# Leftover rows of a spectral mixer in four groups of 32 partitions, and a new order of its column products

## The chip, the cores and the metric

The kernel runs on one core of a Trainium2 chip. The metric is the device time of one execution in microseconds; the time of a kernel is the median over its runs.

## The reference, cut to what matters

```python
x = A_x                                            # [1, 2048, 576], bf16
X = rfft2(layernorm(x), axes=(-2, -1)) * (w_r + 1j * w_i)
h = x + irfft2(X, s=(2048, 576)).astype(bf16)
out = h + (gelu(layernorm(h) @ w_gate) * (layernorm(h) @ w_up)) @ w_down
```

`gelu` is the tanh approximation; `w_gate` and `w_up` are 576 by 4608, `w_down` 4608 by 576. Only the first half, the two-dimensional transform and its inverse, is touched by the change. The second half, the feed-forward network, takes most of the time.

## The kernel before

The 2048 tokens lie as 16 heads h of 128 partitions. All transforms are matmuls with tables that the kernel makes itself. An order written out by hand sets what each engine does: every engine works off its own queue in the order of the program text, and waits where an operand isn't there yet. DMAs are issued by SP's queue. PSUM is one ring of four buffers of two banks each, which all products share (`two`).

**Row transform** (`norms`, `row16`, `rests`). For each head VectorE scales the 128-point row table by the layer norm's 1/std into `FR` (L391), and TensorE multiplies the head's columns by it. The 576 columns are folded into 288 pairs (d, d + 288). `row16` does the pairs 0 to 255 as two full blocks, and adds the mean by a small product with `mneg`. The 32 pairs that are left (columns 256 to 319 and 512 to 575 hold them) go through `rests` (L351): per head two products of 64 columns and two with the mean, in the two halves of the array's columns, 128 wide. `evict` (ScalarE, L361) copies the full blocks of two heads from PSUM to `Bt[:, 0:4]`, `evict4` (L367) the leftovers of four heads to `Bt[:, 4]`, on ScalarE for heads 0 to 7 and on VectorE after that.

**Tables.** `DT` is the column table (sine and cosine, by `col_sin` on ScalarE and `mirror` on VectorE), with block 2 (`D3`) for the leftovers; `DF` is a copy of the parts of it that the leftover products use, with zeros elsewhere. `TF` holds the twiddles (minus sine, cosine, sine) of the second row step, by k. VectorE makes angles (`angle_a`, `angle_b` for the sine, `angle_s`, `angle_c` for the cosine), ScalarE the sine and cosine, VectorE the negated sine. The slice `first` (k = 1, 2) is made early, `rest` (the seven others) after the row transform. `turn_tf` transposes them by DMA into `TI` for the way back; `load_dq` copies `DT` into `DQ` by DMA for the inverse column products.

**Loop over k** (order 1 to 7, then 0). For a column c of the row result, `f2(c)` makes the column products: two output parities, each of three matmuls of 290 columns, two with `DT` and one with `DF` for the leftovers (L550). `f2_out` copies them to `pq` (ScalarE, L561). `f3(k, half)` applies the twiddles to `pq[k]` and `pq[k + 8]` (TensorE L567 and L568, copy to `g` or `hs` on ScalarE L589). `sum_of` (L600) and `wmul` (L618 to L639), both VectorE, form sums and multiply by the spectral weights, giving `Zt`. `i3(k)` is the inverse row product (L658), copied to `EO` by ScalarE. `inv_cols` (L709) and `add_rows` (L848) finish the inverse; then the network's `gate` blocks begin (L978). `wmul` of one k forms the sums of the next k between its own steps.

The order of the loop is software pipelining: step i runs `f2` of its k, `f3` of the k before, `wmul` of the one before that, and `i3` of the third one back. In step 0 the products of k = 1 put the leftover matmuls of both parities last.

Of the kernel before, what the change touches and what calls it, by code (L numbers as in the profile page):

```python
# [20 lines left out]
P = 128  # L21
# [21 lines left out]
def kernel_body(  # L43
# [67 lines left out]
    DF = keep.tile([P, 2, 2, JH], BF16, name="DF")  # L111
# [76 lines left out]
    V.memset(DF[:], 0.0)  # L188
# [18 lines left out]
    iota(iD[64:128, 2:3], [[0, 1]], 2 * P + 64 + 192, 1)  # L207
# [50 lines left out]
    first, rest = slice(0, 2), slice(2, 9)  # L258
# [54 lines left out]
    def fill(dst, n):  # L313

        for _ in range(n):
            T.matmul(dst, lhsT=ident[:], rhs=h_sb[:, 0, 0:512], start=True, stop=True)

    def row16(h):
# [6 lines left out]
        for t in range(2):  # L325
            for n, d0 in ((0, t * P), (1, DH + t * P)):
# [9 lines left out]
                lhsT=mneg[:, 0, h : h + 1].to_broadcast([P, P]),  # L336
# [5 lines left out]
    def rests(h):  # L342
        ps_f["f4", h] = two("f4")
        for i in range(4):
            row16_rest(h + i)

    def row16_rest(h):
        o = (h % 4) * P
        for mean in (False, True):
            for p0, d0 in ((0, 256), (64, 512)):  # L350
                T.matmul(  # L351
                    ps_f["f4", h - h % 4][p0 : p0 + 64, 0, o : o + P],
                    lhsT=mneg[:, 1, h : h + 1].to_broadcast([P, 64]) if mean else h_sb[:, h, d0 : d0 + 64],
                    rhs=FR[:, h, 0, :],
                    start=not mean,
                    stop=mean,
                )
# [8 lines left out]
    def evict4(h):  # L366
        (V.tensor_copy if h >= 8 else A.copy)(  # L367
            Bt[:, 4, :].rearrange("p (c h l) -> p h c l", c=16, h=16)[:, h : h + 4, :, :],
            ps_f["f4", h][:, 0].rearrange("p (h c l) -> p h c l", h=4, c=16),
        )  # L370
# [91 lines left out]
    rests(0)  # L462
# [5 lines left out]
    rests(4)  # L468
# [4 lines left out]
    evict(0, 2)  # L473
    evict4(0)
    evict(4, 6)
    evict4(4)
# [6 lines left out]
    rests(8)  # L483
# [8 lines left out]
    rests(12)  # L492
# [50 lines left out]
    def f2(c):  # L543
# [3 lines left out]
        if c == order[0]:  # L547
            steps.sort(key=lambda s: s[1] == 4)
# [551 lines left out]
```

## Time and profile before

| | us |
|---|---|
| median of 3 runs | 494.45 (494.05 to 494.75) |
| the profiled execution | 494.6 |
| span of its instructions | 492.8 |
| TensorE busy in it | 484.7 |
| VectorE, ScalarE, POOL busy | 223.4, 158.2, 29.5 |
| first column product begins | 21.96 |
| first gate block begins | 65.57 |

The span is the time from the first to the last instruction of the profiled execution. PE is TensorE, DVE VectorE, ACT ScalarE, POOL GpSimd; SPq is the queue that issues DMAs. A line of the order of time gives start, length, engine, line of the kernel, operation, what it writes and reads with its shape, and how many instructions were merged; in brackets stands the idle time ahead of it and what ended that. Matmuls are pipelined, so the lengths of single ones overlap: what one costs in a row of them is the distance from one start to the next. The granted TensorE clock was 1.000 in the whole span.

### The profile page before, as it was taken

What the parts mean: (1) busy time and instruction counts of PE and PEld (TensorE: products, weight loads), DVE (VectorE), ACT (ScalarE), POOL (GpSimd) and SP (SyncE); (2) the same over time, 40 slices, a digit from 0 to 9 for tenths busy, and PEclk for the clock granted to TensorE, in tenths of its full rate; (3) what the DMA queues carried; (4) which work ended last, traced back from release to release, by engine and by line L of the source; (5) the groups of instructions that cost most, each with busy time, mean ns of one, the idle gap of its engine ahead of it and who ended that gap; (6) DMA issues with size and microseconds to landing.
All of it is one profiled execution on the core that took longest, in us unless ns stands there. A gap on an engine that the chain in (4) does not pass through costs nothing.

```text
span 492.8 us, 12868 instructions
## 1 busy us (share of the span) xinstructions
PE 484.7 (98%) x5762; PEld 338.9 (69%) x5762; DVE 223.4 (45%) x457; ACT 158.2 (32%) x280; POOL 29.5 (6%) x84
## 2 busy tenths in 40 slices
PE   6999999999999999999999999999999999999997
PEld 3777789875589955555699755555799655555995
DVE  8999774798622177333311345333121333333111
ACT  8899863322210022332200132332110232232000
POOL 8500010011100011000000000000000000000000
PEclk9999999999999999999999999999999999999999
DMA  8838979769970049966720089876600377760000
GB/s 278 234 74 184 246 115 240 165 128 212 223 161 3 3 118 195 192 145 147 152 65 1 37 170 199 174 145 147 143 3 3 92 158 155 150 146 1 14 13 25
DMA packets 89582, 62.35 MB, mean 127 GB/s; under 512 B 23222, under 2 KB 88118, under 8 KB 89526
## 3 DMA queue, kind: packets, MB, share of 16 engines
q1 hardware_dynamic: 89238, 60.34, 57.5%
q0 software_dynamic: 288, 1.18, 0.7%
q8 instruction: 45, 0.74, 0.7%
q14 instruction: 11, 0.09, 0.1%
HBM read 52.65 MB, written 2.36 MB: 112 GB/s over the span
## 4 chain that ended last, share of the span: by engine, by line
PE 95%; ACT 2%; POOL 1%; DMA 1%; issue 0%; DVE 0%; ACTq 0%; POOLq 0%
PE gu L978 57%; PE acc L1021 27%; PE pq_ps L550 2%; PE cs_ps L709 2%; PE acc L1040 2%; PE eo_ps L658 2%; ACT junk L128 1%; PE y_ps L848 1%; PE gh_ps L568 1%; PE gh_ps L567 1%; DMA h_sb<-in_A_x_dram 1%; POOL rstd L138 1%; ACT Bt L361 0%; POOL wm_r L397 0%; PE eo_ps L682 0%
## 5 line engine op out<-in xcount | busy, mean ns | idle before, releaser
L978 PE MATMUL gu<-Bt,wgu 64*128 64x512 bf16 (+1 forms) x2646 | 270.6, 363 | 0.0
L978 PEld LDWEIGHTS <-wgu 64*128 64x128 bf16 x2646 | 151.5, 94 | 115.6 <-issue 0.3
L987 DVE TENSOR_TENSOR P_sb<-g_sb,gu 128x512 bf16<-128x512 f32 (+1 forms) x156 | 100.4, 645 | 140.3 <-ACT g_sb L986 140.3
L986 ACT ACTIVATE g_sb<-gu 128x512 f32<-128x512 f32 (+1 forms) x156 | 88.0, 564 | 193.5 <-PE gu L978 193.5
L1021 PEld LDWEIGHTS <-P_sb 64*128 64x128 bf16 x2160 | 122.2, 94 | 10.9
L1021 PE MATMUL acc<-wd,P_sb 64*128 64x288 bf16 x1440 | 90.9, 283 | 0.0
L1030 DVE TENSOR_TENSOR part<-part,acc 128x576 f32<-128x576 f32 x15 | 11.3, 754 | 112.6 <-ACT part L1029 112.6
L1029 ACT COPY part<-acc 128x576 f32<-128x576 f32 x15 | 9.6, 639 | 122.8 <-PE acc L1021 122.8
L1021 PE MATMUL acc<-wd_a,P_sb 64*128 64x288 bf16 x720 | 46.8, 283 | 0.0
L550 PE MATMUL pq_ps<-DT,Bt 128*128 128x290 bf16 x64 | 12.3, 286 | 0.7 <-ACT Bt L361 0.7
L978 PE MATMUL gu<-Bt,wgu_e 64*128 64x256 bf16 (+1 forms) x162 | 12.5, 305 | 0.0
L873 DVE TENSOR_SCALAR hrow<-h_sb,mv,rstd 128x1152 bf16<-128x1152 bf16 x14 | 12.2, 868 | 0.6 <-POOL rstd L911 0.6
L138 POOL TENSOR_TENSOR rstd<-rstd,mhalf 128x1 f32<-128x1 f32 (+2 forms) x17 | 12.0, 709 | 1.4
L1032 DVE TENSOR_TENSOR h_sb<-h_sb,part 128x576 bf16<-128x576 bf16 x15 | 11.4, 758 | 0.5
L550 PEld LDWEIGHTS <-Bt 128*128 128x128 bf16 x96 | 9.1, 97 | 3.4 <-ACT Bt L361 0.8
L978 PEld LDWEIGHTS <-wgu_e 64*128 64x128 bf16 x162 | 10.3, 94 | 1.2
L137 POOL TENSOR_SCALAR rstd<-mv 128x1 f32<-128x1 f32 (+2 forms) x17 | 4.1, 242 | 116.7 <-DVE mv L123 116.0
L561 ACT CAST pq<-pq_ps 128x580 bf16<-128x580 f32 x16 | 10.5, 666 | 1.2 <-PE pq_ps L550 1.1
L709 PE MATMUL cs_ps<-DQ,EO 58*128 58x290 bf16 x144 | 10.8, 283 | 0.0
L327 PE MATMUL f2t<-FR,h_sb 128*128 128x256 bf16 x64 | 9.2, 273 | 0.6 <-DVE FR L391 0.6
L709 PEld LDWEIGHTS <-EO 58*128 58x128 bf16 x160 | 7.8, 94 | 2.4 <-issue 0.7
L550 PE MATMUL pq_ps<-DF,Bt 128*128 128x290 bf16 x32 | 8.9, 285 | 0.0
(149 smaller groups left out, 283.9 us busy)
## 6 DMA issues: line engine op xcount, KB each, us to landing
wgu<-in_B_w_gate_dram SPq DMA_DIRECT2D x46, 432.0 KB, 5.1
wgu<-in_B_w_up_dram SPq DMA_DIRECT2D x46, 432.0 KB, 6.1
wd_a<-in_B_w_down_dram SPq DMA_DIRECT2D x1, 1728.0 KB
wd<-in_B_w_down_dram SPq DMA_DIRECT2D x1, 1728.0 KB
wd<-in_B_w_down_dram SPq DMA_DIRECT2D x6, 288.0 KB, 7.9
out_dram<-h_sb SPq DMA_DIRECT2D x3, 576.0 KB
h_sb<-in_A_x_dram SPq DMA_DIRECT2D x4, 288.0 KB, 4.3
h_sb<-in_A_x_dram SPq DMA_DIRECT2D x2, 576.0 KB
```

What stands on the lines that cost most here:

```text
L138: G.tensor_tensor(dst[:, sl], dst[:, sl], mhalf[:, sl], ALU.pow)
L550: T.matmul(ps[:, par, 0:JP], lhsT=Bt[:, t, col], rhs=DT[:, t // 2, par] if t < 4 else DF[:, par], start=(t == par), stop=(t == 4),)
L561: copy(pq[c][:, rs].rearrange("p r (j a) -> p r j a", a=2), pq_ps[c][:, :, 0:JP].rearrange("p a (r j) -> p r j a", r=2)[:, rs],)
L658: T.matmul(pv[:, n], lhsT=z[:, a, w].rearrange("p b j -> p (b j)"), rhs=TI[:, ts[k], 1 - a : 3 - a, :], start=(a == 0), stop=(a == 1),)
L709: T.matmul(ps[:, e, 0:JP], lhsT=EO[x][rows, w, 2 * g : 2 * g + 2].rearrange("p h e k l -> p (h e k l)"), rhs=DQ[rows, w] if w or e else DT ...
L873: V.tensor_scalar(hrow[:], h_sb[:, h, :].rearrange("p (r k) -> p r k", k=64).unsqueeze(2).to_broadcast([P, NR, 2, 64]), mv2[:, h, 0:1], rs ...
L978: T.matmul(gu[:, c, 0:n], lhsT=w[rows, r, i * P : (i + 1) * P], rhs=hl[tcnk % 2][rows, r, lo:hi], start=(r == 0), stop=(r == NR - 1),)
L986: A.activation(g_sb, gu[:, 0, 0:n], ACT.Gelu_apprx_tanh)
L987: V.tensor_tensor(p_sb(f)[:, lo:hi], g_sb, gu[:, 1, 0:n], ALU.mult)
L1021: T.matmul(accs[i][:, c, 0:DH], lhsT=p_sb(f)[rows, st * P : (st + 1) * P], rhs=wd[f // NWA][rows, f % NWA, c * DH : (c + 1) * DH], start=( ...
L1030: V.tensor_tensor(part, part, accs[1][:, :, 0:DH], ALU.add)
L1032: V.tensor_tensor(hv, hv, part, ALU.add)
```

## The change

Leftovers. `rests` now does eight heads at a time and is called twice, after heads 0 to 7 and after 8 to 15. Per head and column parity it forms the 32 leftover pairs in 32 partitions, so that (e, parity) with e = 0 for k and e = 1 for k + 8 fills four groups of 32 partitions; each product is 32 columns by 64. `Bt[:, 4]` keeps half its width; `evict4` copies eight heads at once. `DF` is gone: `D3` holds the same 32 rows in each group. The two last rows of the column table, which `DQ` needs, come from three small ScalarE activations into `edge`, and reach `DQ` by a DMA of their own in each `load_dq`.

Column products. `f2(k)` now does k and k + 8: eight full matmuls, then four leftover matmuls of 32 rows each, one in each group of partitions. For the first k, 32 matmuls of 32 columns are put ahead; `f2` overwrites what they write. 

Order. The products of the first two k come before the first `f3`; then those of the next two before the first `wmul`. From then on a step is `f3`, `f2` of the next k, `i3` of two k back, `wmul`. The late twiddles are made in two parts, k = 3, 4, 5 and k = 6, 7, 0, 8, with the sine and cosine of the second part later and its negated sine inside the first `wmul`. The negation of `G16` moves behind the last `wmul`.

```diff
     V.memset(mhalf[:], -0.5)
-    neg = keep.tile([P, 2], FP32, name="neg")
-    for i in range(2):
-        V.memset(neg[:, i : i + 1], -2.0 + i)
-    mneg = keep.tile([P, 2, H], BF16, name="mneg")
+    mneg = keep.tile([P, H], BF16, name="mneg")
...
     D3 = DT[:, 2]
-    DF = keep.tile([P, 2, 2, JH], BF16, name="DF")
+    edge = Bt[0:2, 4, 8 * P : 8 * P + 4 * JH].rearrange("p (r a j) -> p r a j", r=2, a=2)
     DQ = keep.tile([P, NW, 2, JH], BF16, name="DQ")
...
     def minus_means(lo, hi):
-        sh = [P, 2, hi - lo]
-        G.tensor_tensor(
-            mneg[:, :, lo:hi],
-            mv[:, lo:hi, 0].unsqueeze(1).to_broadcast(sh),
-            neg[:].unsqueeze(2).to_broadcast(sh),
-            ALU.mult,
-        )
+        G.tensor_scalar(mneg[:, lo:hi], mv[:, lo:hi, 0], -2.0, None, op0=ALU.mult)
...
-    V.memset(DF[:], 0.0)
+    for t, b in ((edge[:, 0, 0], hpib), (edge[:, 0, 1], nhpib), (edge[:, 1].rearrange("p a j -> p (a j)"), zerob)):
+        A.activation(t, zerob[0:2].to_broadcast(list(t.shape)), ACT.Sin, bias=b[0:2])
     V.memset(DT[:, :, 1, :, JH - 1], 0.0)
...
     iota(iD[:], [[P, 3]], 0, 1)
-    iota(iD[64:128, 2:3], [[0, 1]], 2 * P + 64 + 192, 1)
+    for p0 in (32, 64, 96):
+        iota(iD[p0 : p0 + 32, 2:3], [[0, 1]], 2 * P, 1)
     iJ = tmp("iJ", [P, 2 * JM], FP32)
...
                 f2t[:, b, t * 2 * P : t * 2 * P + P],
-                lhsT=mneg[:, 0, h : h + 1].to_broadcast([P, P]),
+                lhsT=mneg[:, h : h + 1].to_broadcast([P, P]),
                 rhs=FR[:, h, 0, :],
...
-    def rests(h):
-        ps_f["f4", h] = two("f4")
-        for i in range(4):
-            row16_rest(h + i)
-    def row16_rest(h):
-        o = (h % 4) * P
-        for mean in (False, True):
-            for p0, d0 in ((0, 256), (64, 512)):
-                T.matmul(
-                    ps_f["f4", h - h % 4][p0 : p0 + 64, 0, o : o + P],
-                    lhsT=mneg[:, 1, h : h + 1].to_broadcast([P, 64]) if mean else h_sb[:, h, d0 : d0 + 64],
-                    rhs=FR[:, h, 0, :],
-                    start=not mean,
-                    stop=mean,
-                )
+    def rests(h0):
+        ps = ps_f["f4", h0] = two("f4")
+        for h in range(h0, h0 + 8):
+            o = (h - h0) * 64
+            F = FR[:, h].rearrange("p s (x e n) -> p s x e n", x=2, e=2)
+            for n in range(3):
+                for e in range(2):
+                    for par in range(1 if n == 2 else 2):
+                        p0 = 64 * e + 32 * par
+                        T.matmul(
+                            ps[p0 : p0 + 32, 0, o : o + 64],
+                            lhsT=mneg[:, h : h + 1].to_broadcast([P, 32])
+                            if n == 2
+                            else h_sb[:, h, 256 + DH * n : 288 + DH * n],
+                            rhs=F[:, par if n == 1 else 0, :, e],
+                            start=(n == 0),
+                            stop=(n == 2 - par),
+                        )
...
     def evict4(h):
-        (V.tensor_copy if h >= 8 else A.copy)(
-            Bt[:, 4, :].rearrange("p (c h l) -> p h c l", c=16, h=16)[:, h : h + 4, :, :],
-            ps_f["f4", h][:, 0].rearrange("p (h c l) -> p h c l", h=4, c=16),
+        (V.tensor_copy if h else A.copy)(
+            Bt[:, 4, 0 : 8 * P].rearrange("p (c h l) -> p h c l", c=8, h=H)[:, h : h + 8],
+            ps_f["f4", h][:, 0].rearrange("p (h c l) -> p h c l", h=8, c=8),
         )
...
     norms(0, 4)
-    rests(0)
     minus_sine(first)
...
     norms(4, 8)
-    rests(4)
+    rests(0)
     ln_fin(slice(9, 12, 2))
...
     gather(1)
-    evict(0, 2)
+    evict(0, 2, 4, 6)
     evict4(0)
-    evict(4, 6)
-    evict4(4)
     sd(12, 13)
...
     norms(8, 12)
-    rests(8)
     sd(14, 15)
...
     norms(14, 16)
-    rests(12)
+    rests(8)
     evict(8, 10)
...
     evict4(8)
-    V.tensor_copy(DF[0:32], D3[0:32])
-    V.tensor_copy(DF[96:128], D3[96:128])
-    evict4(12)
     for w, t in ((WR, wm[0]), (WI, wm[1])):
         nc.sync.dma_start(w[:, 9 : H + 1, 0:J], t[:].rearrange("p (r j) -> p r j", r=8))
-    angle_a(rest)
-    angle_b(rest)
+    part_a, part_b = slice(2, 5), slice(5, 9)
+    angle_a(part_a)
+    angle_b(part_a)
+    sine(part_a)
+    angle_s(part_a)
+    angle_c(part_a)
+    minus_sine(part_a)
+    angle_a(part_b)
+    angle_b(part_b)
+    angle_s(part_b)
+    angle_c(part_b)
     for w in (WR, WI):
...
             j0, j1 = w * JW, (w + 1) * JW
-            for lo, hi in ((j0, min(j1, (j0 // P + 1) * P)), ((j0 // P + 1) * P, j1)):
+            for lo, hi in ((j0, min(j1, (j0 // P + 1) * P)), ((j0 // P + 1) * P, min(j1, DH))):
                 if lo < hi:
...
                     )
+        p0 = 64 * r + DH % JW
+        nc.sync.dma_start(DQ[p0 : p0 + 2, NW - 1], edge[:, r])
...
-    def f2(c):
-        ps = two("pq_ps")
-        col = slice(slot[c] * P, (slot[c] + 1) * P)
-        steps = [(par, t) for par in range(2) for t in (par, par + 2, 4)]
-        if c == order[0]:
-            steps.sort(key=lambda s: s[1] == 4)
-        for par, t in steps:
-            T.matmul(
-                ps[:, par, 0:JP],
-                lhsT=Bt[:, t, col],
-                rhs=DT[:, t // 2, par] if t < 4 else DF[:, par],
-                start=(t == par),
-                stop=(t == 4),
-            )
-        pq[c] = wk.tile([P, 2, JP], BF16, name="pq", tag="pq", bufs=6)
-        pq_ps[c] = ps
+    def f2(k):
+        cc = (k, k + 8)
+        for c in cc:
+            ps = pq_ps[c] = two("pq_ps")
+            if c == order[0]:
+                for _ in range(32):
+                    T.matmul(ps[:, 0, 0:32], lhsT=ident[:], rhs=h_sb[:, 0, 0:32], start=True, stop=True)
+            for par in range(2):
+                for t in (par, par + 2):
+                    T.matmul(
+                        ps[:, par, 0:JP],
+                        lhsT=Bt[:, t, slot[c] * P : (slot[c] + 1) * P],
+                        rhs=DT[:, t // 2, par],
+                        start=(t == par),
+                        stop=False,
+                    )
+            pq[c] = wk.tile([P, 2, JP], BF16, name="pq", tag="pq", bufs=6)
+        for e, c in enumerate(cc):
+            col = (slot[c] // 8 * 4 + slot[c] % 4) * P
+            for par in range(2):
+                rows = slice(64 * e + 32 * par, 64 * e + 32 * par + 32)
+                T.matmul(
+                    pq_ps[c][:, par, 0:JP],
+                    lhsT=Bt[rows, 4, col : col + P],
+                    rhs=D3[rows, par],
+                    start=False,
+                    stop=True,
+                )
...
         times(WI, m2, slice(0, J))
+        if i == 1:
+            minus_sine(part_b)
         if k:
...
-    n = len(order)
-    for i in range(n + 1):
-        last = i >= n
-        if not last:
-            f2(order[i])
-            if i != 1:
-                f2_out(order[i])
-        if i == 0:
-            f2(order[0] + 8)
-            f2_out(order[0] + 8)
-            angle_s(rest)
-            angle_c(rest)
-            sine(rest)
-        if 1 <= i <= n:
-            f3(order[i - 1], 0)
-            f3(order[i - 1], 1)
-            if i == 1:
-                f2_out(order[1])
-                minus_sine(rest)
-                sum_of(order[0], 0)
-                sum_of(order[0], 1)
-                V.tensor_scalar(G16v[1], G16v[0], -1.0, None, op0=ALU.mult)
-            else:
-                if i == 2:
-                    cosine(slice(2, 3))
-                elif i == 3:
-                    turn_tf(slice(2, 4))
-                    turn_tf(slice(4, 9))
-                    load_dq(0)
-                    pre = [load_gu(g) for g in range(3)]
-                    nc.sync.dma_start(wd_a[:], wd_view[:, 0:NWA, :])
-                wmul(order[i - 2], i - 1, order[i - 1])
-        if not last and i:
-            f2(order[i] + 8)
-            f2_out(order[i] + 8)
-            if i == 2:
-                cosine(slice(3, 9))
-        if last:
+    def both_out(k):
+        f2_out(k)
+        f2_out(k + 8)
+    o = order
+    f2(o[0])
+    both_out(o[0])
+    f2(o[1])
+    f2_out(o[1])
+    f3(o[0], 0)
+    f2_out(o[1] + 8)
+    f3(o[0], 1)
+    cosine(part_a)
+    turn_tf(part_a)
+    sum_of(o[0], 0)
+    sum_of(o[0], 1)
+    f3(o[1], 0)
+    f3(o[1], 1)
+    sine(part_b)
+    for j in (2, 3):
+        f2(o[j])
+        both_out(o[j])
+    wmul(o[0], 1, o[1])
+    f3(o[2], 0)
+    f3(o[2], 1)
+    cosine(part_b)
+    turn_tf(part_b)
+    load_dq(0)
+    pre = [load_gu(g) for g in range(3)]
+    nc.sync.dma_start(wd_a[:], wd_view[:, 0:NWA, :])
+    scr_pool.__exit__(None, None, None)
+    eop = ctx.enter_context(tc.tile_pool(name="eop", bufs=1, side="right"))
+    EO = [eop.tile([P, 5, H, 2, 4, 8], BF16, name=f"EO{x}", tag=f"EO{x}") for x in range(2)]
+    for s in range(3):
+        i3(o[0], s)
+    wmul(o[1], 2, o[2])
+    for j in range(3, 8):
+        f3(o[j], 0)
+        f3(o[j], 1)
+        if j < 7:
+            f2(o[j + 1])
+            both_out(o[j + 1])
+        else:
             inv_cols(0, 0)
             inv_cols(0, 1)
-        if i >= 3:
-            for s in range(3):
-                i3(order[i - 3], s)
-        if last:
-            wmul(order[i - 1], i)
-        if i == 2:
-            scr_pool.__exit__(None, None, None)
-            eop = ctx.enter_context(tc.tile_pool(name="eop", bufs=1, side="right"))
-            EO = [eop.tile([P, 5, H, 2, 4, 8], BF16, name=f"EO{x}", tag=f"EO{x}") for x in range(2)]
+        for s in range(3):
+            i3(o[j - 2], s)
+        wmul(o[j - 1], j, o[j])
+    wmul(o[7], 8)
+    V.tensor_scalar(G16v[1], G16v[0], -1.0, None, op0=ALU.mult)
     for g in (2, 3, 4):
```

More of the change, by code (lines that the diff above doesn't have):

```diff
@@ L256, in first_a @@
             G.tensor_scalar(pr[:, k], q16[:], s2p[:, 0:1], ks[:, k : k + 1], op0=ALU.mult, op1=ALU.add)
-    first, rest = slice(0, 2), slice(2, 9)
+    first = slice(0, 2)
     first_a()
@@ L315, in fill @@
         for _ in range(n):
-            T.matmul(dst, lhsT=ident[:], rhs=h_sb[:, 0, 0:512], start=True, stop=True)
+            T.matmul(dst[:, 0:512], lhsT=ident[:], rhs=h_sb[:, 0, 0:512], start=True, stop=True)
     def row16(h):
```

## The prediction

> **What bounds the kernel now.** I read the page's busy line first, then the chain of waits, then the stretch that the change rewrites by windows, then each engine's order of time there. All times are microseconds from the span's start.
>
> ```profile
> PE 484.7 (98%) x5762; PEld 338.9 (69%) x5762; DVE 223.4 (45%) x457; ACT 158.2 (32%) x280; POOL 29.5 (6%) x84
> ```
>
> Over the span TensorE is the bound. The change touches only the first 55 us, and these rows show that stretch: the chain (start, length, what), then one window (length; busy time of PE, its weight loads, DVE, ACT, POOL), then VectorE's order of time.
>
> ```profile
> 28.08 1.48 PE pq_ps L550 x12
> 38.06 0.74 PE pq_ps L550 x6
> 38.80 1.09 PE eo_ps L658 x10
> 41.62 0.74 PE pq_ps L550 x6
> 48.01 1.35 PE cs_ps L709 x20
> 49.36 1.20 PE eo_ps L658 x10
> 65.57 27.46 PE gu L978 x468
> ...
> 28.00:48.00 20.00, 19.93 (x167) 15.76 (x167) 20.00 (x46) 19.59 (x35) 0.00 (x0) 1.00 0.68 137
> ...
> 31.07 0.76 DVE L618 TENSOR_TENSOR m<-xab,WR 128x1156 bf16<-128x1156 bf16 x1
> 34.64 0.76 DVE L618 TENSOR_TENSOR m<-xab,WR 128x1156 bf16<-128x1156 bf16 x1
> 48.92 0.76 DVE L618 TENSOR_TENSOR m<-xab,WR 128x1156 bf16<-128x1156 bf16 x1
> ```
>
> The whole-kernel share misleads here. From 28 to 48 TensorE, VectorE and ScalarE are all full. TensorE needs 41.62 - 38.06 = 3.56 for one k; VectorE needs 34.64 - 31.07 = 3.57 for the multiplication of one k and never waits. TensorE finishes each k just behind VectorE: the multiplication of k=6 ends at 48.92 and its inverse product starts at about 49.3 (49.36 in the chain). So a shorter TensorE step shortens the kernel by that lag, 0.3 to 0.4, and no more, unless VectorE also starts earlier.
>
> **Leftover products of the row transform.**
>
> ```profile
> 15.27 0.22 PE L351 MATMUL f<-FR,h_sb 128*64 128x128 bf16 x2
> 15.33 0.22 PE L351 MATMUL f<-FR,mneg 128*64 128x128 bf16 x2
> 15.48 0.39 PE L327 MATMUL f2t<-FR,h_sb 128*128 128x256 bf16 x2
> ...
> 20.22 0.22 PE L334 MATMUL f2t<-FR,mneg 128*128 128x128 bf16 x1
> 20.28 0.38 PE L327 MATMUL f2t<-FR,h_sb 128*128 128x256 bf16 x2
> 20.50 0.22 PE L334 MATMUL f2t<-FR,mneg 128*128 128x128 bf16 x1
> 21.96 0.67 PE L550 MATMUL pq_ps<-DT,Bt 128*128 128x290 bf16 x4 [0.68 <-ACT Bt L361]
> ...
> 19.98 1.93 ACT L361 CAST Bt<-f2t 128x1024 bf16<-128x1024 f32 x2
> ...
> 19.10 0.48 DVE L391 TENSOR_SCALAR FR<-F,rstd 128x256 bf16<-128x256 bf16 x2
> ...
> 47.94 0.29 PE L709 MATMUL cs_ps<-DT,EO 58*128 58x290 bf16 x1
> 47.95 0.80 PE L709 MATMUL cs_ps<-DQ,EO 58*128 58x290 bf16 x9
> ```
>
> A pair in two column halves, 128 columns each, costs 0.06; leaving that mode costs 0.15 - 0.06 = 0.09. Four heads cost 8 x 0.06 + 0.09 = 0.57. After the change eight heads have 24 turns of 64 columns, up to four matmuls each. If four run together as two do (47.94 and 47.95 begin 0.01 apart), a turn is half of 0.06 and a set takes 24 x 0.03 + 0.09 = 0.8. If each of its 80 matmuls takes the 0.03 that one of a pair takes, it is 80 x 0.03 = 2.4. I take 0.8, because the rows show matmuls in different parts starting together; 2.4 is the upper end.
>
> Rows 14 and 15 wait for FR at 19.10, not for TensorE, so the last row product still begins at 20.50. Then comes the second set, 20.65 to 21.4. ScalarE's last row evictions still end at 21.9 (19.98 + 1.93): they wait for row 15. The 32 new small matmuls stand in TensorE's queue ahead of the first column product and wait for nothing. Today there is 0.68 of idle time there to take them. Each streams 32 columns: from 0.014 (1.48 / 12 = 0.123 for 290 columns, scaled) to 0.055 (20.28 - 20.22, a full matmul with its own weight load), so 0.45 to 1.8 in all. I take 0.027 each, half of the upper row, since the streaming is a quarter and the weight load stays: 0.85. The first column product then begins at 21.4 + 0.85 = 22.3, 0.3 later than 21.96 (ends: 0 and +1.2).
>
> **Products of k and k+8 together.** Per k, 12 steps of 0.123 (1.48) become 8 (0.99) and one turn of four matmuls in four row groups. Changing the array's mode costs 1.35 - 10 x 0.123 = 0.12 going in (20 matmuls in pairs), and 1.20 - 1.09 = 0.11 coming out. By the first rows above it is 0.09; I take 0.18 for both ways. Run together, the turn costs 0.12 + 0.18 = 0.30 and a k saves 0.19, 1.5 over eight. Run one by one it is 0.49 + 0.18 and a k loses 0.18. I take the saving. The Trainium skill, "TensorE: Matmul & The Clock Gate", section "Measured speedup vs the span model", gives 3.07 times for four row groups, not 4; by that the turn would cost an estimated 0.04 more, which changes TensorE's work and not the sum below.
>
> **VectorE, which then decides.**
>
> ```profile
> 20.54 0.68 DVE L367 CAST Bt<-f 128x512 bf16<-128x512 f32 x1
> 21.13 0.29 DVE L500 COPY DF<-DT 32x580 bf16<-32x580 bf16 x1
> ...
> 21.77 0.69 DVE L367 CAST Bt<-f 128x512 bf16<-128x512 f32 x1
> 22.50 1.15 DVE L245 SCALAR_TENSOR_TENSOR pr<-q,s2p,ks 128x896 int32<-128x896 f32 x1
> 23.68 0.63 DVE L269 TENSOR_SCALAR pr<-pr 128x896 int32<-128x896 int32 x1
> 24.34 0.73 DVE L272 TENSOR_SCALAR ab<-pr 128x896 f32<-128x896 int32 x1
> 25.11 0.63 DVE L232 TENSOR_SCALAR ab<-ab 128x896 int32<-128x896 int32 x1
> 25.66 0.42 DVE L284 TENSOR_SCALAR TF<-TF 128x896 bf16<-128x896 bf16 x1
> 25.99 1.41 DVE L600 TENSOR_TENSOR xab<-g,gh_ps 128x578 bf16<-128x578 bf16 x2
> 27.32 0.22 DVE L760 TENSOR_SCALAR G<-G 128x256 bf16<-128x256 bf16 x1
> 27.49 0.77 DVE L618 TENSOR_TENSOR m<-xab,WR 128x1156 bf16<-128x1156 bf16 x1
> ...
> 25.29 0.62 ACT L589 CAST g<-gh_ps 128x578 bf16<-128x578 f32 x1
> ```
>
> Gone before the first multiplication are the two DF copies (21.77 - 21.13 = 0.64), one eviction (0.73) and the negation of G (0.17), about 1.5. But the eviction of the leftovers stands first in this queue, and it moves from 20.54 to 21.6, behind the second set. It takes 0.6; the angles, 25.66 - 22.50 = 3.16 in four passes, become eight half passes and one short minus-sine, about 3.7 with their extra starts. VectorE is free for the sums at 21.6 + 0.6 + 3.7 = 25.9, as before (25.99).
>
> The sums also need the first g. TensorE: 22.3, the column products of k=1, 9 and of k=2, 10 (2 x 1.29, from 0.99 + 0.30), the first half of the twiddle product of k=1 (4 x 0.123): 25.4. ScalarE copies it with 0.2 of latency and 0.53 (25.29 to the next start at 25.82): the sums begin at about 26.2 and the first multiplication at 26.2 + 1.33 = 27.5, no earlier than 27.49. In it now stands the minus-sine of the late part (0.26), which needs ScalarE's late sine. ScalarE's queue ahead of it: g to 26.1, the copy of 10, an early cosine (0.5 by its columns), g and hs of k=2, then 0.6 of sine, ending near 29.1, while the second multiplication ends at 27.5 + 1.35 = 28.85. VectorE waits 0.3 and then works 0.26: every later k is 0.5 to 0.6 later on VectorE. TensorE, 0.19 per k shorter, takes back the lag of 0.3 but also ends its last k with a change of mode. **Sum**: +0.55 - 0.3 = +0.25 if all the lag is used, +0.55 if none; I take +0.4.
>
> **Hidden edits.**
>
> ```profile
> 5.98 0.46 DVE L384 BATCH_NORM_STATS2 st<-h_sb 128x6 f32<-128x288 bf16 x1 [0.52 <-DMA h_sb<-in_A_x_dram]
> ...
> 9.72 0.27 POOL L137 TENSOR_SCALAR rstd<-mv 128x4 f32<-128x4 f32 x1 [0.48 <-DVE FR L391]
> ...
> 33.41 4.44 SPq L518 DMA_DIRECT2D DQ<-DT  x6
> ```
>
> Three edge activations on ScalarE delay the first row table by about 0.2; VectorE's wait of 0.52 for input at 5.98 hides it. Two more iotas on POOL, some 0.4, lie ahead of a wait of 0.48 at 9.72; without that cover they would cost 0.4. Two edge DMAs of about 0.74 each (4.44 / 6), and a late twiddle transpose waiting for its cosine, move SP's weight loads by some 4; their first use is at 65.57.
>
> **Rivals.**
> *Leftovers one by one* (slower). The second set takes 2.4 and the first delays rows 8 to 11 by 1.6: the second set ends near 23.9, the leftovers' eviction and the first column product come 2.5 later, +2.9: 497.5. It decides from the point where a matmul of 32 columns by 64 costs over 0.015. For it: no row here shows four column groups. Against it: the pair at 47.94. The Trainium skill, "TensorE: Matmul & The Clock Gate", section "Wait — 56ns, not 53.3ns?", states that start to start never drops below about 25 ns however small N is; by that rule this rival would hold, and the pairs of this trace contradict it for different parts of the array. Chance 0.15.
> *Small matmuls at full price* (slower). 32 x 0.055 = 1.8: the column products begin at 23.2 and the sum is +1.3: 495.9. Against it: three quarters of their streaming is gone. Chance 0.2; smaller delays of the leftovers' eviction end here too.
> *TensorE's saving counts* (faster). If VectorE were free earlier, 8 x 0.19 less: 493.1. For it: 1.5 of VectorE's work before the first multiplication is gone. Against it: 20.00 of 20.00 busy, and nothing removed from its 3.57. Chance 0.1.
> *The change does nothing to the path*: TensorE's lag pays for the late minus-sine, 494.6; part of the forecast.
>
> **How the numbers follow.** The profiled execution took 494.6 with a span of 492.8; the median shown is 494.45, 0.15 less. So 494.6 + 0.4 = 495.0, or 494.9 as a median. About 0.2% (1.0) is what a measurement of this kernel tells from no change. The forecast (chance 0.55) has its own range of 494.3 to 495.5, nearly all of it within 0.2%. With the rivals the range is 494.0 to 497.4. Slower by over 0.2%: 0.15 + 0.2 and a little of the forecast, 0.42. Faster by over 0.2%: 0.1. Within: 0.48.
>
> **What would show it.** Right: VectorE still full from 28 to 48 at 3.57 per k, with small TensorE waits on it; the first column product at 22.0 to 22.4; a VectorE wait for ScalarE's late sine. Wrong: a second leftover set over 1.2 long, a step per k other than 3.57, or a first multiplication before 27.

## The result, and the profile after

| | before | after |
|---|---|---|
| median, us (lowest to highest, 7 runs each) | 494.55 (494.05 to 494.75) | 496.06 (495.67 to 496.67) |
| profiled execution, us | 494.6 | 496.67 |
| span, us | 492.8 | 494.9 |

The ratio is 1.0033, with a 95% interval of 1.0021 to 1.0045: slower by 1.5 us. The forecast was 494.9, with a range of 494.0 to 497.4 that holds the result. The forecast's own part of that range ended at 495.5 and doesn't hold it.

The page of after (busy time of each engine) shows what the whole-kernel view can: almost nothing.

```profile
PE 484.0 (98%) x5890; PEld 336.9 (68%) x5890; DVE 222.4 (45%) x456; ACT 159.4 (32%) x283; POOL 29.7 (6%) x86
```

TensorE has 0.7 less work than before and the kernel is 1.5 slower. The profiled execution must also be read with care. In the order of time of after, VectorE waits for an input transfer:

```profile
6.84 0.46 DVE L379 BATCH_NORM_STATS2 st<-h_sb 128x6 f32<-128x288 bf16 x1 [1.43 <-DMA h_sb<-in_A_x_dram]
```

The same row stood at 5.98 before, and stands between 5.45 and 6.02 in the twelve later profiles. The scaling of the last two heads' rows, L386, is late by the same: 20.00 instead of 19.10. So some 0.9 of this profile's span is a late transfer of this one execution. The kernel was therefore profiled once more, unchanged (below: after, again). There the last two heads' rows are scaled at 19.10, as in the profile of before, so the two can be laid side by side. Its order of time, TensorE first, then VectorE, ScalarE and POOL:

```profile
20.50 0.22 PE L327 MATMUL f2t<-FR,mneg 128*128 128x128 bf16 x1
20.64 0.24 PE L344 MATMUL f<-FR,h_sb 128*32 128x64 bf16 x8
...
21.32 0.20 PE L344 MATMUL f<-FR,mneg 128*32 128x64 bf16 x2
21.46 0.96 PE L548 MATMUL pq_ps<-h_sb,ident 128*128 128x32 bf16 x32
22.27 1.15 PE L551 MATMUL pq_ps<-DT,Bt 128*128 128x290 bf16 x8
23.35 0.30 PE L563 MATMUL pq_ps<-DT,Bt 32*128 32x290 bf16 x4
23.59 1.16 PE L551 MATMUL pq_ps<-DT,Bt 128*128 128x290 bf16 x8
...
24.91 0.30 PE L578 MATMUL gh_ps<-pq,TF 128*128 128x289 bf16 x1
...
19.10 0.48 DVE L386 TENSOR_SCALAR FR<-F,rstd 128x256 bf16<-128x256 bf16 x2
21.57 0.69 DVE L362 CAST Bt<-f 128x512 bf16<-128x512 f32 x1 [0.79 <-PE f L344]
22.18 0.61 DVE L238 SCALAR_TENSOR_TENSOR pr<-q,s2p,ks 128x384 int32<-128x384 f32 x1
22.82 0.53 DVE L262 TENSOR_SCALAR pr<-pr 128x384 int32<-128x384 int32 x1
...
26.39 1.42 DVE L611 TENSOR_TENSOR xab<-g,gh_ps 128x578 bf16<-128x578 bf16 x2
27.90 0.77 DVE L629 TENSOR_TENSOR m<-xab,WR 128x1156 bf16<-128x1156 bf16 x1
...
29.34 0.29 DVE L277 TENSOR_SCALAR TF<-TF 128x512 bf16<-128x512 bf16 x1
31.77 0.76 DVE L629 TENSOR_TENSOR m<-xab,WR 128x1156 bf16<-128x1156 bf16 x1
...
25.70 0.64 ACT L600 CAST g<-gh_ps 128x578 bf16<-128x578 f32 x1
...
22.59 0.45 POOL L505 TENSOR_SCALAR WR<-WR 128x34 bf16<-128x34 bf16 x1 [3.47 <-DMA WR<-wm_r]
```

Against the rows of before, in us:

| | before | after, again | later by |
|---|---|---|---|
| first column product | 21.96 | 22.27 | 0.31 |
| first copy of g | 25.29 | 25.70 | 0.41 |
| first multiplication | 27.49 | 27.90 | 0.41 |
| second multiplication | 31.07 | 31.77 | 0.70 |
| inverse row product of k = 6 | 49.30 | 50.28 | 0.98 |
| last matmul begins | 489.50 | 490.46 | 0.96 |
| span | 492.81 | 494.05 | 1.24 |

Four steps make up the 1.24 but for rounding: 0.41 ahead of the first multiplication, 0.29 between the first and the second (3.87 instead of 3.58), 0.27 that TensorE falls further behind VectorE, and 0.28 behind the last matmul. Of the 0.41, some 0.09 is this execution's own: POOL's scaling of WR falls on two of VectorE's angle instructions (L262 0.53, the next one 0.45, each 0.36 in the first profile of after). In that first profile the first multiplication comes 8.71 behind the scaling of the last rows, here 8.80, before 8.39. The medians differ by 1.4 to 1.5; what they have beyond the 1.24 isn't placed by these two profiles.

The steady part of after, again, is as full as before, by windows, and by the chain of waits (start, length, what; one step):

```profile
28.00:48.00 20.00, 19.21 (x164) 13.46 (x163) 20.00 (x45) 19.33 (x35) 0.00 (x0) 1.00 0.57 107
```

```profile
43.16 1.20 PE eo_ps L671 x10
44.36 0.12 PE gh_ps L578
44.48 0.23 PE gh_ps L579
...
45.46 1.04 PE pq_ps L551 x8
46.50 0.23 PE pq_ps L563 x4
46.73 1.20 PE eo_ps L671 x10
```

VectorE is busy 20.00 of 20.00 again. A TensorE step is 46.73 - 43.16 = 3.57, as before (3.56): 1.20 + 1.10 + 1.27, with 0.11 of waiting in the second twiddle product (0.23 instead of 0.12).

The last 0.28 lies behind everything. In the waits of SP's queue near the end (line, releaser: us, times, longest), before first, then after:

```profile
SPq L1095 <- DMA out_dram<-h_sb: 0.9, 1, 0.9
```

```profile
SPq L1108 <- DMA out_dram<-h_sb: 1.2, 1, 1.2
```

The last output transfer is issued at 490.31 of 492.81 before and at 492.10 of 494.89 after: 2.50 and 2.79 to the end. The transfers use eight semaphores in turn, 154 transfers before and 156 after. At the end SP waits for these semaphores and four others in six pairs, in a fixed order, 0.06 apart by the trace's semaphore events. Before, the last transfer's semaphore is in the sixth pair, and the other five are gone through while it is under way. After, it is in the first pair, and the five others follow behind the long wait.

### The profile page after: what moved, and what is told of

Read it like the earlier page. It is cut to its first block, busy times and chain, and to the rows that moved or that the text cites. A ratio compares the mean times of both kernels' runs of the same rounds, so it can differ in the third digit from the quotient of the medians.

```text
span 494.9 us, 13128 instructions
## 1 busy us (share of the span) xinstructions
PE 484.0 (98%) x5890; PEld 336.9 (68%) x5890; DVE 222.4 (45%) x456; ACT 159.4 (32%) x283; POOL 29.7 (6%) x86
## 4 chain that ended last, share of the span: by engine, by line
PE 94%; POOL 2%; DMA 1%; ACT 1%; DVE 1%; issue 0%; SPq 0%; POOLq 0%; ACTq 0%
PE gu L991 57%; PE acc L1034 27%; PE cs_ps L722 2%; PE acc L1053 2%; PE pq_ps L551 2%; PE eo_ps L671 2%; PE y_ps L861 1%; DMA h_sb<-in_A_x_dram 1%; POOL rstd L135 1%; PE gh_ps L579 1%; ACT pq L572 0%; PE gh_ps L578 0%; PE pq_ps L563 0%; PE eo_ps L695 0%; POOL wm_r L392 0%
## 5 line engine op out<-in xcount | busy, mean ns | idle before, releaser
L551 PE MATMUL pq_ps<-DT,Bt 128*128 128x290 bf16 x64 | 9.2, 286 | 0.4 <-ACT EO L679 0.4
L671 PE MATMUL eo_ps<-TI,Zt 128*128 128x256 bf16 x70 | 8.8, 273 | 0.3 <-ACT pq L572 0.3
L579 PE MATMUL gh_ps<-pq,TF 128*128 128x289 bf16 x32 | 8.2, 286 | 0.7 <-ACT pq L572 0.7
```

The lines of the kernel that those rows point to most:

```text
L551: T.matmul(ps[:, par, 0:JP], lhsT=Bt[:, t, slot[c] * P : (slot[c] + 1) * P], rhs=DT[:, t // 2, par], start=(t == par), stop=False,)
L579: T.matmul(dst, lhsT=TF[:, ts[k1], t1, :], rhs=b, start=False, stop=True)
L671: T.matmul(pv[:, n], lhsT=z[:, a, w].rearrange("p b j -> p (b j)"), rhs=TI[:, ts[k], 1 - a : 3 - a, :], start=(a == 0), stop=(a == 1),)
```

## The experiments

All times beside the kernel before on the same chip; its median was 494.43 in the first four, 494.3 in the next four, 494.62 in the last four. "Behind the last pair of rows" means counted from the scaling of heads 14 and 15.

**No small matmuls.** The loop of 32 is left out.

> The changed kernel without the 32 small matmuls ahead of the first column product; nothing that the outputs need is left out. Theory (they stand in the way): in the profile of the changed kernel they run from 22.36 to 23.17 and the last row eviction ends at 22.96, so the first column product begins about 0.2 earlier and the time falls by 0.2 to 0.3, to about 495.8. Rival (they are only in the gap, and the first sums hang on VectorE's angles, which begin after the leftovers' eviction): no change, 496.06 within 0.1.

Measured 495.88, ratio 1.0031 (1.0022 to 1.0041). Behind the last pair of rows the first column product comes at 3.03 instead of 3.17, the first multiplication at 8.65 instead of 8.80. So the 32 cost 0.14 and no more; the first column product then waits for ScalarE's last eviction. (3.17 and 8.80 are those of after, again; against the first profile's 8.71 the first multiplication gains 0.06.) The median is within 0.2 of after's two, 496.06 and 495.99, too little to tell.

**Late minus-sine on POOL.** `minus_sine(part_b)` leaves the first `wmul`; `G.tensor_scalar` does it after `sine(part_b)`.

> The changed kernel with the negated sine of the late part made by POOL instead of VectorE inside the first multiplication. Theory (VectorE paces the loop and this step stands in its way): in the changed kernel the step from the first to the second multiplication is 32.59 - 28.71 = 3.88 against 3.57 for all others; it becomes 3.57, and the time falls by 0.3 to 495.75. Rival (TensorE paces the loop): the VectorE step shrinks and the time stays at 496.06 within 0.1.

Measured 496.18 (1.0021 to 1.0045 times before): nothing gained. The order of time shows why:

```profile
29.79 1.67 POOL L768 TENSOR_SCALAR TF<-TF 128x512 bf16<-128x512 bf16 x1 [2.72 <-ACT TF L271]
30.01 0.87 DVE L634 TENSOR_TENSOR za<-m,m 128x580 bf16<-128x580 bf16 x1
30.80 0.45 DVE L635 TENSOR_TENSOR zb<-m,m 128x580 bf16<-128x580 bf16 x1
```

Beside POOL a VectorE instruction that takes 0.45 elsewhere takes 0.87; the next one, also inside POOL's 1.67, takes its 0.45. The step from the first to the second multiplication is 3.99, no shorter than 3.87.

**Edges by memset.** The three early ScalarE activations become `V.memset`.

> The changed kernel with the two edge rows set by three memsets on VectorE instead of three activations on ScalarE at the start. In the profile of the changed kernel VectorE waits for input until 6.84 against 5.98 before, and the first scaling of the row table is 0.86 later. Theory (the early edits delay the input): that wait ends near 6.0 again and the time falls by 0.6 or more, to 495.4. Rival (the late input was the chance of one execution): the time stays within 0.15 of 496.06, and where the wait ends differs from run to run.

Measured 495.95 (1.0021 to 1.0048 times before): the early edits cost nothing that shows. This run's profile holds the same meeting of POOL and VectorE by chance:

```profile
22.21 0.66 POOL L505 TENSOR_SCALAR WR<-WR 128x34 bf16<-128x34 bf16 x1 [3.27 <-DMA WR<-wm_r]
22.64 0.81 DVE L262 TENSOR_SCALAR pr<-pr 128x384 int32<-128x384 int32 x1
```

L262 takes 0.36 when alone (first profile of after). The meeting moved the sine, the copies of the column products and the first multiplication to 9.06. Whether it happens hangs on when WR lands.

**Column products of the next k ahead of the twiddle products**, in the steady loop:

```diff
-        f3(o[j], 0)
-        f3(o[j], 1)
         if j < 7:
             f2(o[j + 1])
             both_out(o[j + 1])
+        f3(o[j], 0)
+        f3(o[j], 1)
```

> The changed kernel with the column products of the next k ahead of the twiddle products again in the steady steps, the rest as it is. Theory (TensorE keeps its lag behind VectorE because the twiddle product waits for the copies of the pair that was just made): the waits of about 0.15 per step at the twiddle products go, the inverse product of k=6 begins within 0.3 of the end of its multiplication (0.55 in the changed kernel), and the time falls by 0.2 to 0.3, to 495.8. Rival (the order doesn't matter, since VectorE sets 3.57 per step and the lag arises in the last step): within 0.1 of 496.06; or slower, if the copies of g and hs now come later than VectorE needs them.

Measured 495.93 (1.0017 to 1.0037 times before). The lag of TensorE behind VectorE fell from 0.65 to 0.13, but VectorE now waits once for its operand:

```profile
36.90 0.47 DVE L611 TENSOR_TENSOR xab<-g,hs 128x578 bf16<-128x578 bf16 x1 [0.30 <-ACT hs L600]
```

From the third to the seventh multiplication it needs 14.75 instead of 14.29. Lag and wait are the same time, moved.

**Six more output transfers**, to turn the order of the eight semaphores that the transfers use in turn back to that of before. The three transfers of four heads go out in pieces of 2, 1 and 1 heads.

> The kernel after, with the three output transfers of four heads each cut into three pieces, so that six more transfers are issued on SP's queue, the last of them some 100 us before the end. Theory A (the tail): the span goes on 3.30 us after the last matmul in the kernel after and 3.02 in the kernel before, since SP waits at the end for the transfers' semaphores one pair after another, 0.06 us apart; the two transfers that the change adds turn the order of eight semaphores by two, so that the last transfer's stands in the first pair and five waits follow it. Six more make eight, the old order: 3.02 us from the last matmul to the end, one long wait just ahead of SP's last step, and 0.28 us less than the kernel after, about 495.8 beside 494.5 of before. Rival B: the longer tail belongs to something else: 3.30 us stay, and the time is that of the kernel after, 496.06, or later by what six issues of 0.6 us cost, nothing.

**Two more output transfers in the kernel before**, its first two cut in half.

> The kernel before, with the first two output transfers of four heads cut in two, so two more transfers and nothing else. Theory A (the tail): 3.3 us instead of 3.02 from the last matmul to the end, with the long wait first and five short ones behind it; 0.28 us more than before, about 494.75 beside 494.5, a ratio of 1.0006, small beside its interval, so the tail in the profile decides. Rival B: 3.02 us and no change.

The tail does what theory A says in both, with 162 and 156 transfers in all. Waits of SP's queue, with six more, then before with two more:

```profile
SPq L1109 <- DMA out_dram<-h_sb: 0.9, 1, 0.9
```

```profile
SPq L1096 <- DMA out_dram<-h_sb: 1.2, 1, 1.2
```

From the last issue to the end it is 2.49 (494.48 - 491.99) and 2.78 (492.79 - 490.01). So the tail belongs to the number of transfers, not to anything else in the change. The medians don't show it: 494.53 for before with two more (0.9989 to 1.0010 times before), an interval wider than 0.28; and 496.38 for the other (1.0027 to 1.0055), where 495.8 was expected, more than after, for another reason. TensorE's order of time in that run, in the first leftover set:

```profile
15.69 0.19 PE L344 MATMUL f<-FR,mneg 128*32 128x64 bf16 x1 [0.38 <-issue]
...
16.45 0.25 PE L344 MATMUL f<-FR,h_sb 128*32 128x64 bf16 x6 [0.52 <-issue]
```

TensorE stands twice, 0.57 and 0.72 from start to start, and waits for nothing that the profile names. The last head's row products are still 0.7 late. The next two runs, on the same chip, have it too, so they are compared with this one.

**First angles ahead of the last leftover eviction.** `angle_a(part_a)` moves ahead of `evict4(8)`.

> The kernel after, with the first angle instruction of the twiddles' first part (0.61 us on VectorE) put ahead of the eviction of the second leftover set, where VectorE waits 0.79 us for the set. The sine of that part stands on ScalarE ahead of the copies of the first column products, and it waits 1.2 us for VectorE's angles; in two of the runs so far GpSimd's scaling of WR ran beside the second angle instruction and that took 0.80 us instead of 0.36, and the first multiplication came 9.06 us behind the last pair of rows instead of 8.71. Theory A (the late sine holds the copies): the sine starts about 0.6 us earlier, the copies follow the column products at once, the first multiplication comes 0.1 to 0.2 us earlier than in the kernel after (8.5 to 8.6 us behind the last pair of rows) and the 0.35 us of the unlucky runs goes too: 0.1 to 0.4 us less in the median, 495.7 to 495.95. Rival B (TensorE sets the first copy of g: two pairs of column products, 2.65 us, stand ahead of the first twiddle products where three column products of 0.74 stood): the first multiplication stays at 8.7 us, 496.05.

Measured 496.78 (1.0034 to 1.0061). Counted from row 15's last product, the first multiplication comes at 7.61, as with six more transfers (7.61); the 0.28 of the tail is the rest of the difference but for 0.1. VectorE gave its time back as a wait:

```profile
27.31 1.43 DVE L611 TENSOR_TENSOR xab<-g,gh_ps 128x578 bf16<-128x578 bf16 x2 [0.68 <-ACT g L600]
```

Rival B holds here: the first g sets the sums, and g hangs on two pairs of column products. In the run that it is compared with, VectorE waited 0.27 for g already. With the short gap there is as little to gain: in after, again, the copy of g ends at 26.34 and the sums begin at 26.39.

**Late twiddles in one part**, angles, sine and minus-sine of all seven together, where the kernel before has them.

> The kernel after, with the late twiddles' angles, their sine and minus-sine in one part of 128x896 again, placed as in the kernel before; the cosines and the turns stay in two parts. Theory A (the two parts cost): the late minus-sine no longer stands behind the first multiplication, so the first step from multiplication to multiplication takes 3.57 us and not 3.88; VectorE has 0.8 us less of fixed costs; the sine of 1.04 us stands on ScalarE between the copies of the first and the second pair and holds the third copy by about 0.5 us, which the first twiddle product doesn't need. About 0.3 us less than the kernel after, 495.75. Rival B: the minus-sine of 0.42 us and the longer angle instructions stand ahead of the first sum, which comes later by as much as the first step gains: 496.05, with the first multiplication 9.0 us behind the last pair of rows.

Measured 497.24 (1.0043 to 1.0070). Beside the run with six more transfers (496.38) that is 0.86 more, 0.28 of it the tail. The step to the second multiplication falls to 3.58 as theory A says, but the first one comes 0.63 later:

```profile
27.76 1.42 DVE L604 TENSOR_TENSOR xab<-g,gh_ps 128x578 bf16<-128x578 bf16 x2 [0.65 <-ACT g L593]
```

The long sine stands ahead of the third copy and of g on ScalarE. In this order of products the two parts are worth 0.6 and cost 0.3.

**After, again**, unchanged.

> The kernel after, unchanged, beside the next three on one chip. In the last three kernels built on it TensorE stood twice inside the first leftover set, 0.57 and 0.72 us, with nothing in the profile that it waited for, and the first column product came 4.14 us behind the last pair of rows; in the profile of after and in the four runs before those the same place cost one gap of 0.19 to 0.22 us, and the column product came at 3.0 to 3.2. Theory A (the chip or the place of the program decides): this run shows the same gap as the other three of its call that leave the place as it is. Rival B (chance of one execution): the gaps differ from kernel to kernel within the call. Time 496.05 with the short gap, 496.7 with the long ones.

Measured 495.99 (1.0017 to 1.0036). The gap in the first set is the short one, 0.20, as in the next run, in after's first profile and in the first four experiments (0.19 to 0.22). Long gaps were seen in three runs, all on one chip, and nowhere else; what makes them long stays open.

**The program's packets moved.** TensorE's program comes into the core in packets (the last section has the row). The 12 matmuls of 512 columns that stand ahead of the first head's products (`FILL`) become 96 of 64 columns, so all that follows moves by 168 instructions.

> The kernel after with the 12 matmuls of 512 columns that run ahead of the first head's products cut into 96 of 64, of about the same length in all: 168 more rows of TensorE's program ahead of the leftover sets. The trace shows the program coming in by packets of 16 KB (256 rows of 64 bytes), and the gaps always at about the 70th of the first set's 80 matmuls, some 270 rows from the program's start. Theory A (the gap is a border between two such packets, reached while the 32x64 products eat 160 rows in 0.7 us): the border moves ahead of the set, among the 128x256 products, where it is hidden; the first set runs without a gap, 0.70 us; its leftovers are evicted 0.2 us earlier, or 1.2 us earlier where the gaps are long. The time is the same as that of after where the gap is short (496.05; the set is not on the path then), and 0.5 to 0.7 us below it where they are long. Rival B (the gap belongs to the products themselves or to what they wait for): it stays at the 70th matmul of the set, and the time is that of after.

Measured 496.95 (1.0028 to 1.0059). The gap stays at the 70th matmul of the set, 0.20: theory A falls for it. But the trace shows a new stall, far off, in the inverse column products:

```profile
57.72 0.29 PE L722 MATMUL cs_ps<-DQ,EO 58*128 58x290 bf16 x1
58.53 0.68 PE L722 MATMUL cs_ps<-DQ,EO 58*128 58x290 bf16 x8 [0.52 <-issue]
```

From 57.72 to 58.53 it stands 0.7 longer than a start there takes, and what comes behind keeps it: the gate blocks begin 14.17 behind the eighth multiplication, 13.49 in after, again. The profiled execution is not the odd one: its span, 495.2, lies inside the 494.5 to 495.7 of the seven, against 493.8 to 494.7 in after, again.

**The kernel before with leftover sets of eight.** Only the places of `rests` and the order of the evictions change.

> The kernel before, with its leftover sets of four heads moved to where the change has its sets of eight: both sets of the first eight heads behind head 7's rows, both of the last eight behind head 15's, nothing else. Theory A (the late place is what delays the first column product and VectorE): 16 more products of 64 rows x 128 columns, 0.056 us each or half of it where two row groups run together, so 0.45 to 0.9 us more of TensorE ahead of the first column product, which waits for the evictions anyway (0.05 us of slack); VectorE's evictions, now both behind the last set, start 1.0 us later, and the first multiplication comes 0.4 to 0.8 us later: 495.0 to 495.3 beside 494.5. Rival B (the late place is hidden by the evictions of the last heads' rows): within 0.1 us, 494.5.

Measured 495.61 (1.0011 to 1.0033). Behind the last pair of rows the first multiplication comes at 9.36 instead of 8.39, 0.97 later. Order of time:

```profile
20.89 0.69 DVE L367 CAST Bt<-f 128x512 bf16<-128x512 f32 x1 [0.55 <-PE f L351]
22.24 0.69 DVE L367 CAST Bt<-f 128x512 bf16<-128x512 f32 x1
...
22.99 0.42 PE L549 MATMUL pq_ps<-DF,Bt 128*128 128x290 bf16 x2 [0.64 <-DVE Bt L367]
```

Theory A holds, with more than its 0.4 to 0.8, and the median is above its 495.3: VectorE waits for the set, its second eviction ends at 22.93, and TensorE's first leftover column product waits for that, a wait that the expectation didn't name.

**What the runs suggest, together**: no small matmuls; leftovers in four places of four heads; first angles early; six more transfers; fills of 44 by 140 columns.

> The kernel after with what the runs so far suggest: no small matmuls, leftover products in four places of four heads each as in the kernel before (still in four groups of 32 partitions), the first angles ahead of the last eviction of leftovers, six more output transfers, and the first fills cut into 44 of 140 columns, which puts the border of the program's packets outside the leftover sets. By the sum of what was seen: 0.14 us and 0.15 to 0.3 for an earlier first column product, 0.1 for the earlier sine, 0.28 for the tail, 0 to 0.7 for the border, against the kernel after; the late minus-sine (0.3 us) and the longer lag of TensorE (0.27 us) stay. 495.1 to 495.5, so still behind the kernel before at 494.4. Rival: the stages between set the pace anew, and only the tail's 0.28 shows: 495.75.

Measured 495.25 (1.0002 to 1.0023 times before). Order of time:

```profile
18.92 0.48 DVE L389 TENSOR_SCALAR FR<-F,rstd 128x256 bf16<-128x256 bf16 x2
21.04 0.69 DVE L365 CAST Bt<-f 128x512 bf16<-128x512 f32 x1 [0.22 <-PE f L347]
25.68 1.43 DVE L613 TENSOR_TENSOR xab<-g,gh_ps 128x578 bf16<-128x578 bf16 x2 [0.21 <-ACT g L602]
27.19 0.77 DVE L631 TENSOR_TENSOR m<-xab,WR 128x1156 bf16<-128x1156 bf16 x1
31.07 0.76 DVE L631 TENSOR_TENSOR m<-xab,WR 128x1156 bf16<-128x1156 bf16 x1
```

The first multiplication is at 8.27 behind the last pair of rows, 0.53 ahead of after, again, and 0.12 ahead of before; the tail is the short one. These 0.53 and 0.28 are the 0.8 gained over after, again; which of the four edits gave the 0.53 isn't separated. The step to the second multiplication is still 3.88 and the lag still 0.65: these 0.3 and 0.27, less the 0.12, make 0.45 of the 0.6 by which the median stays behind before. No version tried beats the kernel before.

## Why the prediction was right or wrong

The number lies in the range by luck: the range was wide for two rivals that did not happen, the forecast's own part ended at 495.5, the sum said +0.4, and the two comparable profiles say +1.24. By its steps:

- **Leftover products.** Right. The second set runs from 20.64 to 21.34, 0.70 for 24 turns, 0.029 each (predicted 0.03, with 0.8 in all). The four groups start some 0.003 apart. The rival *leftovers one by one* is dead.
- **First column product at 22.3.** Right: 22.27, with 0.025 for a small matmul (predicted 0.027). The rival *small matmuls at full price* is dead too, though its 495.9 is the nearest figure. By the Trainium skill, "TensorE: Matmul & The Clock Gate", section "Wait — 56ns, not 53.3ns?", starts don't come closer than about 25 ns; the 32 full-height small matmuls agree (0.81 / 32), the four groups don't.
- **The first multiplication "at 26.2 + 1.33 = 27.5"** failed, by 0.4 (0.3 without POOL's chance meeting). TensorE and ScalarE were 0.1 later than the step had it (g at 25.70, not 25.6), the copy of g held the sums for its whole 0.64 and some latency, not 0.53, and the 1.33 for the sums came from counting the negation of G as time of its own. From the first sum to the multiplication it takes 1.51 with that negation gone (27.90 - 26.39), and 1.50 with it (27.49 - 25.99): it ran inside the end of the sums. VectorE's own chain came to the same moment, and not at "25.9": its angles and short minus-sine take 26.39 - 22.18 = 4.21, of which the meeting with POOL is 0.26, instead of 3.7. Freeing VectorE gains nothing (the run with early angles).
- **Products of k and k + 8 together, "a k saves 0.19"**: nearly right in size, and not usable. From start to start a pair takes 23.59 - 22.27 = 1.32 instead of 1.48, both changes of mode in it, so 0.16 are saved. The twiddle products give it back: the second one waits 0.11 for ScalarE's copies (19.33 of 20.00 busy), and a step is 3.57 again.
- **"TensorE takes back the lag of 0.3"** failed in sign. The lag from the start of a multiplication to the inverse product of the k before it is 0.65 in the last step instead of 0.38. Most of the difference is there early. One row of before, then those of after, again, one step behind the second multiplication and at the end:

```profile
35.08 1.25 PE L658 MATMUL eo_ps<-TI,Zt 128*128 128x256 bf16 x10
...
34.63 1.15 PE L551 MATMUL pq_ps<-DT,Bt 128*128 128x290 bf16 x8 [0.43 <-ACT EO L679]
35.95 1.26 PE L671 MATMUL eo_ps<-TI,Zt 128*128 128x256 bf16 x10
50.28 1.26 PE L671 MATMUL eo_ps<-TI,Zt 128*128 128x256 bf16 x10
...
35.34 0.76 DVE L629 TENSOR_TENSOR m<-xab,WR 128x1156 bf16<-128x1156 bf16 x1
49.63 0.76 DVE L629 TENSOR_TENSOR m<-xab,WR 128x1156 bf16<-128x1156 bf16 x1
...
32.74 0.75 ACT L274 ACTIVATE TF<-ab,nhpib 128x512 bf16<-128x512 f32 x1
33.57 1.01 ACT L679 CAST EO<-eo_ps 128x1024 bf16<-128x1024 f32 x1
```

  At the third multiplication the lag is 35.95 - 35.34 = 0.61 already, before 35.08 - 34.64 = 0.44. TensorE waits 0.43 there for ScalarE's copy of the first inverse product, which stands behind the late cosine of the second part in ScalarE's queue. That the cosine makes this wait is read from the order of the queue; no run moves it alone. The three steps that follow leave the lag at 0.6, since the twiddle products' wait eats what is saved, while before takes back 0.03 of its lag. In the last step there are no column products and so no saving, and the lag grows by 0.05, where before takes back another 0.03. The prediction named the change of mode there and gave neither it nor the late cosine a price.
- **Late minus-sine, 0.3 of waiting and 0.26 of work**: the size was off. ScalarE's sine is there in time (29.34 follows the multiplication at once), and the step grows by 0.29.
- **VectorE full, 3.57 per k**: right, and with it the point that less work for TensorE inside the steady part (19.21 of 20.00 busy instead of 19.93) shortens nothing.
- **The tail, 0.28**: in no part of the prediction. The two edge transfers were counted for their place in SP's queue alone.
- **Hidden edits**: right for the early ones, by the run with memsets.

The 1.5 of work taken off VectorE, which the prediction saw, went to pay for the late set and for longer angles: in the kernel before the set's move alone puts the first multiplication 0.97 later, and in after 0.41 of delay is left. This balance is argued from the two runs; the changed kernel with nothing but its sets moved back was not run.

## What to carry to other kernels

Where three engines are full at the same step length, taking work off one of them moves a wait and no time; price a change there by when the first item of the full engine's chain starts, and follow every copy on the way with its full length. A removed instruction that ran inside the end of its neighbour is worth nothing. Count the transfers that an edit adds up to the end of the kernel too: the last wait can change.

## What the runs showed of the hardware that was not expected

- The final waits of SP go through the transfers' semaphores in a fixed order. Here two transfers more, early in the program or near its end, move the end by 0.28 (2.50 and 2.79 from the last issue to the end); eight more give the old 2.5 again.
- A POOL instruction can hold up one of VectorE's by about its own length, whatever the length of VectorE's: POOL's scaling of WR takes 0.40 alone, and an angle instruction that met it took 0.81 instead of 0.36 (edges by memset), 1.07 instead of 0.63 (late twiddles in one part) and 0.87 instead of 0.43 (the last run). The Trainium skill, "SBUF — State Buffer", section "SBUF: two separate sides", calls the port pair that the two share an exclusive lock, which whichever starts first has for its whole instruction; these rows fit that. POOL's late minus-sine doesn't quite: its row is 1.67 long, and only the first VectorE instruction inside it is held.
- TensorE may run out of program; this is not shown. In the page of after (queue: packets, MB, share):

```profile
q8 instruction: 46, 0.75, 0.7%
```

That is 16 KB a packet. The Trainium skill, "Runtime: NRT & Kernel Launch", section "Instruction fetch mechanics", has the same blocks, of 256 instructions, and says that crossing from one to the next is mostly hidden. Here 168 instructions more at the start, of about equal length in time, brought a stall of 0.7 with no named cause nearly 50 us later. That the packets make it is argued from their new times (11.03, 17.31 and 24.49 instead of 16.20, 22.54 and 28.06), not shown.
- One input transfer held VectorE until 5.45 to 6.02 in thirteen profiles and until 6.84 in one; that profile alone would have charged 0.9 of it to the change.
